# Low parts, decays and an ELU step change engines and tiles while float64 weights are narrowed

## The chip, the core and the metric

The kernel runs on one core of one Trainium2 chip. The core has five engines that run their own instruction lists in order: TensorE (PE in the profile, with its weight loads as PEld), VectorE (DVE), ScalarE (ACT), GpSimd (POOL) and SyncE (SP, which here only starts transfers). They meet at semaphores. The metric is the device time of one execution in microseconds (us), as the median of several runs.

## The reference, cut to what matters

Three stages follow each other: retention attention with a decay per head, a dense feed-forward layer with ELU, and a routed feed-forward layer with eight experts.

```python
for t in range(S):                                   # B=4, H=8, S=768, D=64
    state = gamma * state + einsum('bhd,bhe->bhde', k[:, :, t], v[:, :, t])
    y[:, :, t] = scale * einsum('bhd,bhde->bhe', q[:, :, t], state)
h = x @ w_in                                         # 3072x512 @ 512x2048, w_in is float64
g = np.where(h > 0.0, h, np.exp(np.minimum(h, 0.0)) - 1.0)
x2 = (g @ w_out).astype(np.float32)                  # 2048x512, w_out is float64
...
logits = x2 @ w_gate                                 # then a greedy assignment, 384 tokens per expert
out[mask] = np.maximum(x2[mask] @ w1[e], 0.0) @ w2[e]
```

## The kernel before, in words

**Attention in units.** The tokens are cut into 24 units: one batch and one chunk of 128 tokens each, chunk 0 of all four batches first (units 0 to 3), then chunk 1 (units 4 to 7), and so on. Per unit SP loads `qk` and `kv`; `decays` multiplies the queries by `gq` (a power of gamma that rises with the token) and the values by `gk` (the inverse power); PE computes the scores `sc`; `masks` multiplies them by the triangle `tri` into `A`; `attend` forms `py` from A and the values, and for later chunks from the state `st`; `carry` forms `pu` from keys and values and VectorE adds it to `st`. `y_out` splits `py` into a high part `yH` (ACT) and a low part `yL` (VectorE).

**Blocks.** Two units make a block of 256 tokens, numbered n from 0 to 11. For a block and each of 8 slices i of the hidden layer PE computes the first product `ph` (24 matmuls, named phn_i below), and ACT and VectorE turn it into ELU: ACT forms Relu(-h) and Exp of its negative in `e`, then 1 is subtracted, then VectorE takes max(h, 0) + e. ACT and VectorE (or POOL) split it into `gH` and `gL`, and PE accumulates the second product `px` (12 matmuls for a slice). Every product uses three passes, high x high, high x low, low x high.

**Weights.** w_in and w_out arrive as float64 in 16 slices of two pieces (`rw`, 512 KB each); the order of the slices is w1 0, w1 1, w2 0, w1 2, w2 1, and so on. Per piece `scales` multiplies the upper words (ACT mostly), `narrow` builds a float32 out of the two words in three VectorE instructions over a tile `n_rw` (shift left, and/or, shift right/or), `highs` rounds it into `w1H` or `w2H` on ACT, and `lows` subtracts that into `w1L` or `w2L`. Before the change the third narrowing step writes into `rw` itself, with a stride of two words, and the high and low steps read it there.

**Order.** No loop sets the order. Each of these functions is a generator that names, ahead of each instruction, the engine or a choice of engines with a cost in ns, the tiles it needs and a condition; a planner with its own clock for each engine repeatedly takes the instruction that can start first, with ranks to break ties, and emits it. What an engine executes is therefore one fixed list. The first weights are needed by block 0 and 1 while they are narrowed. Once all lows are out, the weight stage's tiles are released, the gate weights `wgb` are loaded into their place, and VectorE gets a further load that fills its gaps: `junk` (dot products of finished rows with the gate weights) and `junkw` (the same with summed weights `wsum`). Routing and the experts follow after the last block.

All engine calls pass through one wrapper, so the profile gives nearly every instruction the line L201; tiles tell them apart.

Of the kernel before, what the change touches and what calls it, by code (L numbers as in the profile page):

```python
# [18 lines left out]
OP = mybir.AluOpType  # L19
# [30 lines left out]
def _constants():  # L50
# [10 lines left out]
    tri = (t[:, None] <= t[None, :]).astype(np.float64)  # L61
    gk = gam[None, :] ** (-(t[:, None] + 1.0))
# [226 lines left out]
def body(ctx: ExitStack, tc, qkv, w_in, w_out, w_gate_t, w1, w2, cst, rc, rmat, out, dbg=None):  # L289
# [68 lines left out]
    def decays():  # L358
        for k in range(len(seq)):
            yield on({"DVE": 600 + DEC, "POOL": 1050}, csb, when=lambda: did["unit_load"] > k)  # L360
            u = units[k]
            eng = yield on({"DVE": 600 + DEC, "POOL": 1050}, u["q0"])
            engines[eng].tensor_tensor(u["q0"], u["q0"], gq, op=OP.mult)
# [15 lines left out]
    def scores(k):  # L379
# [6 lines left out]
        yield on("PE", bank_slot(spare_tag()), csb, when=lambda: did["decay_q"] > k)  # L386
# [8 lines left out]
    def masks(k):  # L395
        u = units[k]
        u["A"] = []
        for hh in range(2):
            yield on("DVE", u["sc"][hh], ap.slot(f"A{hh}", 1))
            a = ap.tile([P, NP, P], F32, tag=f"A{hh}", bufs=1, name=f"A{k}_{hh}")  # L400
            DVE.tensor_tensor(a, u["sc"][hh].rearrange("p (a b) -> p a b", a=NP), tri, op=OP.mult)
            u["A"].append(a)

    def attend(k):
        b, c = seq[k]
        yield on("PE", bank_slot(spare_tag()), when=lambda: did["decay"] > k)
# [50 lines left out]
    def attention():  # L457
        ahead = False
        for k in range(len(seq)):
# [3 lines left out]
            ahead = k < 3 and did["decay_q"] > k + 1  # L463
# [9 lines left out]
    stage[1] = Tiles(stage[0].enter_context(tc.tile_pool(name="stg", bufs=2)), plan, 2)  # L473
    win, wout, raws, slim = {}, {}, {}, {}
# [47 lines left out]
    def narrow():  # L522
        for s, (nm, i) in enumerate(slices):
            group = [[0], [1]] if s == 0 else [[0, 1]]
            for cs in group:
                yield on("DVE", when=lambda: did["scaled"] > 2 * s + cs[-1] if wide else did["weight"] > s)
# [14 lines left out]
                for c, r in zip(cs, rs):  # L541
                    slim[(nm, i, c)] = words(r, 0).bitcast(F32)
# [69 lines left out]
    def elus(par):  # L612
        for k in range(par, n_all, 2):
# [707 lines left out]
```

## Time and profile before

| what | value |
|---|---|
| median of 3 runs | 1062.28 us (1062.04 to 1063.79) |
| the profiled execution's own time | 1063.49 us |
| its span in the trace | 1061.7 us, mean granted TensorE clock 0.967 |
| busy: PE / DVE / ACT / POOL | 984.9 / 773.2 / 395.2 / 234.6 us |

The own time is the one the device reports for the profiled execution; the span reaches from its first to its last recorded instruction. Busy time of an engine counts instructions only, including the time that a started instruction is held up. The granted clock is 1.00 at 2.4 GHz and lower where a stretch was partly run at 1.2 GHz.

### The profile page before, as it was taken

How to read it: one execution, taken by the hardware profiler on the slowest of the kernel's cores; microseconds unless marked ns; L12 is line 12 of the kernel's file. 1: busy time of each engine (PE TensorE's matmuls, PEld its weight loads, DVE VectorE, ACT ScalarE, POOL GpSimd, SP SyncE). 2: the span in 40 equal slices, each digit the busy share in tenths (PEclk: the TensorE clock that was granted, in tenths of full speed). 3: DMA queues.
4: the chain of work that ended last, by engine and by line, in shares of the span. 5: the costliest groups of instructions: out<-in, count | busy, mean ns of one | idle time of the engine just before them, and what ended most of it. 6: DMA issues, size and time to landing. Idle time of an engine off the chain costs nothing.

```text
span 1061.7 us, 17628 instructions
## 1 busy us (share of the span) xinstructions
PE 984.9 (93%) x6899; PEld 846.8 (80%) x6899; DVE 773.2 (73%) x1876; ACT 395.2 (37%) x614; POOL 234.6 (22%) x220
## 2 busy tenths in 40 slices
PE   4586999998999999999999999995999999999996
PEld 4475888887888888888888889874878878888995
DVE  4999876998898989894647475557868778877320
ACT  2454423332332332323333334403354453445541
POOL 2557521111112221120201000001041132233221
PEclk9788999999999999899999999997999999999998
DMA  9762141111110303030201000006577677668850
GB/s 312 275 223 75 40 179 61 40 60 41 47 53 5 96 2 99 2 100 1 101 1 61 1 21 2 12 21 211 154 210 199 189 203 214 178 193 248 232 138 34
DMA packets 55971, 115.01 MB, mean 108 GB/s; under 512 B 4176, under 2 KB 28752, under 8 KB 55760
## 3 DMA queue, kind: packets, MB, share of 16 engines
q1 hardware_dynamic: 47440, 84.52, 24.0%
q0 software_dynamic: 8448, 29.37, 11.6%
q8 instruction: 54, 0.88, 0.3%
q14 instruction: 29, 0.24, 0.1%
HBM read 84.51 MB, written 12.58 MB: 91 GB/s over the span
## 4 chain that ended last, share of the span: by engine, by line
PE 63%; DVE 23%; issue 8%; DMA 2%; POOL 2%; ACT 2%; SPq 0%; POOLq 0%; DVEq 0%; ACTq 0%
PE px L201 19%; PE ph L201 17%; PE po L201 9%; PE eh L201 9%; DVE junk L201 6%; DVE n_rw L201 5%; DVE e L201 3%; DVE junkw L201 3%; PE py L201 2%; PE sc L201 2%; DVE gL L201 2%; DVE rw L201 2%; DMA xg<-xd,idx 1%; DVE A L201 1%; PE pt L201 1%
## 5 line engine op out<-in xcount | busy, mean ns | idle before, releaser
L201 PE MATMUL ph<-yH,w1H 128*128 128x256 f32 x768 | 222.9, 290 | 18.8 <-DVE e L201 18.3
L201 PE MATMUL ph<-yH,w1L 128*128 128x256 f32 x768 | 219.1, 285 | 1.9 <-POOL w1L L201 1.9
L201 PE MATMUL ph<-yL,w1H 128*128 128x256 f32 x768 | 218.8, 285 | 0.3 <-DVE yL L201 0.3
L201 PEld LDWEIGHTS ph<-yH,w1H 128*128 128x128 f32 x768 | 148.5, 193 | 24.8 <-DVE e L201 14.3
L201 PEld LDWEIGHTS ph<-yH,w1L 128*128 128x128 f32 x768 | 148.6, 193 | 4.0 <-POOL w1L L201 2.5
L201 PEld LDWEIGHTS ph<-yL,w1H 128*128 128x128 f32 x768 | 148.8, 194 | 0.5 <-DVE yL L201 0.5
L201 PE MATMUL px<-w2H,gH 128*128 128x512 f32 x332 | 135.9, 409 | 4.8 <-ACT gH L201 4.8
L201 PE MATMUL px<-w2H,gL 128*128 128x512 f32 x332 | 132.4, 399 | 4.1 <-DVE gL L201 4.1
L201 DVE SCALAR_TENSOR_TENSOR junk<-x,wgb 128x512 f32<-128x512 f32 x160 | 131.6, 822 | 5.4 <-ACT x L201 1.2
L201 PE MATMUL px<-w2L,gH 128*128 128x512 f32 x332 | 132.4, 399 | 0.0
L201 ACT ACTIVATE e<-ph 128x512 f32<-128x512 f32 x96 | 56.7, 591 | 175.4 <-PE ph L201 174.7
L201 ACT ACTIVATE gH<-e 128x512 fp32r<-128x512 f32 x83 | 52.4, 631 | 122.5 <-DVE e L201 116.7
L201 DVE SCALAR_TENSOR_TENSOR junkw<-wsum,wgb 128x512 f32<-128x512 f32 x128 | 90.2, 705 | 10.5 <-POOL wsum L201 8.3
L201 PE MATMUL eh<-xTL,w1H 128*128 128x384 f32 x256 | 89.2, 349 | 0.5 <-DVE xTL L201 0.5
L201 PE MATMUL eh<-xTH,w1H 128*128 128x384 f32 x256 | 89.7, 350 | 0.0
L201 PE MATMUL eh<-xTH,w1L 128*128 128x384 f32 x256 | 88.1, 344 | 0.0
L201 PEld LDWEIGHTS px<-w2H,gH 128*128 128x128 f32 x332 | 63.2, 190 | 21.9 <-ACT gH L201 5.7
L201 ACT ACTIVATE hH<-eh 128x384 fp32r<-128x384 f32 x64 | 31.3, 490 | 131.0 <-PE eh L201 118.7
L201 PEld LDWEIGHTS px<-w2H,gL 128*128 128x128 f32 x332 | 63.1, 190 | 21.3 <-DVE gL L201 6.2
L201 PE MATMUL po<-w2H,hL 128*128 128x512 f32 x192 | 77.6, 404 | 0.0
L201 PE MATMUL po<-w2H,hH 128*128 128x512 f32 x192 | 77.5, 404 | 0.0
L201 PE MATMUL po<-w2L,hH 128*128 128x512 f32 x192 | 77.4, 403 | 0.0
(170 smaller groups left out, 1847.2 us busy)
## 6 DMA issues: line engine op xcount, KB each, us to landing
e1R<-in_w_dram SPq DMA_DIRECT2D x32, 512.0 KB, 6.5
e2R<-in_w_dram SPq DMA_DIRECT2D x32, 512.0 KB, 4.5
kv<-in_qkv_dram SPq DMA_DIRECT2D x24, 512.0 KB, 5.4
qk<-in_qkv_dram SPq DMA_DIRECT2D x23, 512.0 KB, 5.3
rw<-in_moe_w_in_dram SPq DMA_DIRECT2D x16, 512.0 KB, 10.4
rw<-in_moe_w_out_dram SPq DMA_DIRECT2D x16, 512.0 KB, 8.7
w1L<-e1R POOLq DMA_DIRECT2D x16, 512.0 KB
w2L<-e2R POOLq DMA_DIRECT2D x16, 512.0 KB
```

Of the source, the lines that this page charges most:

```text
L201: r = real(*args, **kw)
```

## The change

Four edits. (1) `lows` runs on VectorE alone, and `scales` may use ACT or VectorE only, and the list that results holds no POOL arithmetic before the decays of unit 8. (2) `decays`: for the first 8 units only VectorE may do it; units of chunk 0 get no decay of the queries at all. Their scores are multiplied by `hmask` instead, a mask per head that holds the triangle times the power of gamma (512 KB, loaded as one transfer), and their values are decayed only after `attend` has read them, for the state. `csb`, which holds gq, gk and tri, is loaded after the first unit. (3) The third narrowing step writes into `n_rw`, which gets four buffers and a condition on finished lows. (4) The subtraction of 1 and the maximum of the ELU become one VectorE instruction, max(e - 1, h).

```diff
+BUSY = 8
+NAR = 4
...
-DEC, LOW = 500, 900
+DEC = 500
...
 def load_units():
             if k == 0:
+                SP.dma_start(hmask, hm)
             SP.dma_start(kv, qkv[b, c][:, 2:])
+            if k == 0:
+                SP.dma_start(csb, cst)
+                SP.dma_start(rcs, rc)
...
 def decays():
-            yield on({"DVE": 600 + DEC, "POOL": 1050}, csb, when=lambda: did["unit_load"] > k)
+            engs = {"DVE": 600} if k < BUSY else {"DVE": 600 + DEC, "POOL": 1050}
+            yield on(engs, csb, when=lambda: did["unit_load"] > k)
+            if c > 0:
+                eng = yield on(engs, u["q0"])
                 engines[eng].tensor_tensor(u["q0"], u["q0"], gq, op=OP.mult)
-            eng = yield on({"DVE": 600 + DEC, "POOL": 1050}, u["v"])
+            eng = yield on(engs, u["v"], when=lambda: c > 0 or did["attended"] > k)
             engines[eng].tensor_tensor(u["v"], u["v"], gk[:, :, None].to_broadcast([P, H, D]), op=OP.mult)
...
 def masks(k):
+            mask = tri if seq[k][1] else hmask[:, hh * NP * P : (hh + 1) * NP * P].rearrange("p (a b) -> p a b", a=NP)
-            DVE.tensor_tensor(a, u["sc"][hh].rearrange("p (a b) -> p a b", a=NP), tri, op=OP.mult)
+            DVE.tensor_tensor(a, u["sc"][hh].rearrange("p (a b) -> p a b", a=NP), mask, op=OP.mult)
...
 def scales():
-                eng = yield on({"ACT": 900, "DVE": 900, "POOL": 1230}, g)
+                eng = yield on({"ACT": 600, "DVE": 600}, g)
...
 def narrow():
+                    and did["low", "w1"] + did["low", "w2"] > 2 * s + cs[-1] - NAR,
-                        o = stage[1].tile(list(r.shape)[:-1], U32, tag="nar", name=f"n_{r.name}")
+                        o = stage[1].tile(list(r.shape)[:-1], U32, tag="nar", bufs=NAR, name=f"n_{r.name}")
-                        DVE.scalar_tensor_tensor(words(r, 0), words(r, 0), 29, o, op0=OP.logical_shift_right, op1=OP.bitwise_or)
+                        DVE.scalar_tensor_tensor(o, words(r, 0), 29, o, op0=OP.logical_shift_right, op1=OP.bitwise_or)
...
 def lows():
-                yield on("POOL", when=lambda: did["high"] > 2 * s + c)
+                yield on("DVE", when=lambda: did["high"] > 2 * s + c)
-                eng = yield on({"POOL": 1230, "DVE": 600 + LOW}, hi)
-                engines[eng].tensor_sub(lo, slim.pop((nm, i, c)), hi.bitcast(F32))
+                DVE.tensor_sub(lo, slim.pop((nm, i, c)), hi.bitcast(F32))
...
 def elus(par):
-            eng = yield on({"ACT": 520, "DVE": 340}, e)
-            if eng == "ACT":
-                ACT.activation(e, e, AF.Copy, bias=-1.0)
-            else:
-                DVE.tensor_scalar(e, e, -1.0, None, op0=OP.add)
             yield on("DVE", e)
-            DVE.scalar_tensor_tensor(e, ph, 0.0, e, op0=OP.max, op1=OP.add)
+            DVE.scalar_tensor_tensor(e, e, -1.0, ph, op0=OP.add, op1=OP.max)
```

Since the planner writes the lists anew, the order changes too. Three places follow; in the names rw100 is slice 0 of w1, piece 0 (rw2 is w2), the figure after sc, py, pu, A, qk and kv is the unit, and the last number only tells buffers apart.

VectorE at the start of the weight stage, from the first narrowing on. Before:

```order
L201 SCALAR_TENSOR_TENSOR n_rw100_93_141<-rw100_93,n_rw100_93_141 128x512
L201 SCALAR_TENSOR_TENSOR rw100_93<-rw100_93,n_rw100_93_141 128x512
L201 TENSOR_SCALAR n_rw101_95_159<-rw101_95 128x512
L201 TENSOR_TENSOR yL0_157<-py0_138,yH0_156 128x4x128
L201 TENSOR_TENSOR st_78<-pu0_165,csb_77 128x256
L201 TENSOR_TENSOR A1_0_181<-sc1_0_126,csb_77 128x512
L201 TENSOR_TENSOR A1_1_183<-sc1_1_127,csb_77 128x512
L201 SCALAR_TENSOR_TENSOR n_rw101_95_159<-rw101_95,n_rw101_95_159 128x512
L201 SCALAR_TENSOR_TENSOR rw101_95<-rw101_95,n_rw101_95_159 128x512
L201 TENSOR_SCALAR n_rw110_97_198<-rw110_97 128x512
L201 TENSOR_SCALAR n_rw111_99_200<-rw111_99 128x512
L201 TENSOR_TENSOR yL0_157<-py1_185,yH0_156 128x4x128
```

VectorE in the changed kernel, from the lows of the second slice to the same yL of unit 1:

```order
L208 TENSOR_TENSOR w1L_1_207<-n_rw110_101_190,w1H_1_206 128x4x128
L208 TENSOR_TENSOR w1L_1_207<-n_rw111_103_193,w1H_1_206 128x4x128
L208 TENSOR_SCALAR n_rw120_109_237<-rw120_109 128x512
L208 TENSOR_SCALAR n_rw121_111_241<-rw121_111 128x512
L208 SCALAR_TENSOR_TENSOR n_rw120_109_237<-rw120_109,n_rw120_109_237 128x512
L208 SCALAR_TENSOR_TENSOR n_rw121_111_241<-rw121_111,n_rw121_111_241 128x512
L208 TENSOR_TENSOR kv1_94<-kv1_94,csb_77 128x512
L208 SCALAR_TENSOR_TENSOR n_rw120_109_237<-rw120_109,n_rw120_109_237 128x512
L208 TENSOR_TENSOR yL0_147<-py1_239,yH0_146 128x4x128
```

The yL of unit 1, which completes the input of block 0, stood in VectorE's list behind two narrowed pieces; now it stands behind six, four lows and two decays of values.

PE ahead of the first product ph0_0 (repeated rows of a group left out). Before:

```order
L201 MATMUL pu0_165<-kv0_85 64x64 x8
L201 MATMUL py1_185<-A1_0_181,kv1_90 64x128
L201 MATMUL py1_185<-A1_1_183,kv1_90 64x128
...
L201 MATMUL pu1_204<-kv1_90 64x64 x8
L201 MATMUL ph0_0_220<-yH0_156,w1H_0_161 128x256
L201 MATMUL ph0_0_220<-yH0_156,w1L_0_162 128x256
L201 MATMUL ph0_0_220<-yL0_157,w1H_0_161 128x256
```

PE in the changed kernel, at the same place:

```order
L208 MATMUL pu0_153<-kv0_84 64x64 x8
L208 MATMUL sc2_0_172<-qk2_163 128x128
L208 MATMUL sc2_1_173<-qk2_163 128x128
...
L208 MATMUL py1_239<-A1_0_167,kv1_94 64x128
L208 MATMUL py1_239<-A1_1_169,kv1_94 64x128
...
L208 MATMUL ph0_0_258<-yH0_146,w1H_0_183 128x256
L208 MATMUL ph0_0_258<-yH0_146,w1L_0_184 128x256
L208 MATMUL pu1_261<-kv1_94 64x64 x8
L208 MATMUL ph0_0_258<-yL0_147,w1H_0_183 128x256
```

The scores of unit 2, whose load qk2 stands in SP's queue behind the first eight weight pieces, now come ahead of py of unit 1, and the first product is split around pu of unit 1.

VectorE at the first ELU. Before:

```order
L201 TENSOR_SCALAR e0_0_284<-e0_0_284 128x512
L201 SCALAR_TENSOR_TENSOR rw120_105<-rw120_105,n_rw120_105_274 128x512
L201 SCALAR_TENSOR_TENSOR e0_0_284<-ph0_0_220,e0_0_284 128x512
L201 SCALAR_TENSOR_TENSOR rw121_107<-rw121_107,n_rw121_107_280 128x512
L201 TENSOR_SCALAR n_rw210_152_332<-rw210_152 128x512
L201 TENSOR_TENSOR gL0_0_327<-e0_0_284,gH0_0_326 128x512
```

And in the changed kernel:

```order
L208 SCALAR_TENSOR_TENSOR e0_0_313<-e0_0_313,ph0_0_258 128x512
L208 SCALAR_TENSOR_TENSOR n_rw210_176_326<-rw210_176,n_rw210_176_326 128x512
L208 SCALAR_TENSOR_TENSOR n_rw211_178_332<-rw211_178,n_rw211_178_332 128x512
L208 TENSOR_TENSOR gL0_0_344<-e0_0_313,gH0_0_343 128x512
L208 SCALAR_TENSOR_TENSOR n_rw210_176_326<-rw210_176,n_rw210_176_326 128x512
```

One VectorE instruction of each ELU is gone; what stands between e and gL is narrowing in both.

## Rows read from the trace of the kernel before

**Rows 1.** The page, busy time, share of the span and instructions of each engine.

```profile
PE 984.9 (93%) x6899; PEld 846.8 (80%) x6899; DVE 773.2 (73%) x1876; ACT 395.2 (37%) x614; POOL 234.6 (22%) x220
```

**Rows 2.** Windows: length, busy of PE, PEld, DVE, ACT, POOL, clock, DMA share, GB/s.

```profile
15.38:17.26 1.88, 1.88 (x22) 1.88 (x24) 1.81 (x4) 0.68 (x1) 0.00 (x0) 1.00 1.11 374
...
22.00:188.05 166.05, 138.61 (x1053) 118.29 (x1053) 144.32 (x218) 71.35 (x121) 75.86 (x50) 0.90 0.42 148
...
45.00:67.00 22.00, 17.89 (x136) 14.59 (x136) 22.00 (x37) 12.55 (x21) 5.98 (x5) 0.89 0.52 167
...
188.05:688.00 499.95, 486.87 (x3652) 430.25 (x3653) 383.01 (x824) 167.84 (x280) 67.08 (x57) 0.99 0.12 39
```

**Rows 3.** DVE's groups between 15 and 125 us: busy us, mean ns | idle before.

```profile
L201 DVE SCALAR_TENSOR_TENSOR n_rw<-rw,n_rw 128x512 uint32<-128x512 uint32 x31 | 30.8, 1020 | 0.0
L201 DVE TENSOR_SCALAR n_rw<-rw 128x512 uint32<-128x512 uint32 x32 | 26.1, 840 | 4.6 <-ACT rw L201 4.0 <-POOL rw L201 0.6
L201 DVE SCALAR_TENSOR_TENSOR rw<-rw,n_rw 128x512 uint32<-128x512 uint32 x30 | 22.7, 777 | 0.1
L201 DVE TENSOR_TENSOR gL<-e,gH 128x512 fp32r<-128x512 f32 x8 | 9.1, 1143 | 1.7 <-ACT gH L201 1.7
L201 DVE TENSOR_SCALAR e<-e 128x512 f32<-128x512 f32 x7 | 6.2, 882 | 0.0
L201 DVE SCALAR_TENSOR_TENSOR e<-ph,e 128x512 f32<-128x512 f32 x9 | 6.1, 679 | 0.2
...
L201 DVE TENSOR_TENSOR w2L<-rw,w2H 128x512 fp32r<-128x512 f32 x2 | 1.3, 679 | 0.0
```

**Rows 4.** Timeline of POOL, then DVE, near 70 us: start, length, instruction.

```profile
69.07 1.23 POOL L201 TENSOR_TENSOR kv<-kv,csb 128x512 f32<-128x512 f32 x1
70.26 1.74 POOL L201 TENSOR_TENSOR w1L<-rw,w1H 128x512 fp32r<-128x512 f32 x1
...
69.31 1.53 DVE L201 SCALAR_TENSOR_TENSOR n_rw<-rw,n_rw 128x512 uint32<-128x512 uint32 x1
70.77 1.79 DVE L201 TENSOR_TENSOR gL<-e,gH 128x512 fp32r<-128x512 f32 x1
```

**Rows 5.** Timeline of DVE at two moments at which POOL runs nothing.

```profile
15.38 0.43 DVE L201 TENSOR_SCALAR n_rw<-rw 128x512 uint32<-128x512 uint32 x1 [4.01 <-ACT rw L201]
...
46.96 0.68 DVE L201 SCALAR_TENSOR_TENSOR rw<-rw,n_rw 128x512 uint32<-128x512 uint32 x1
47.56 0.68 DVE L201 TENSOR_TENSOR gL<-e,gH 128x512 fp32r<-128x512 f32 x1
...
49.37 0.41 DVE L201 TENSOR_SCALAR n_rw<-rw 128x512 uint32<-128x512 uint32 x1
49.70 1.28 DVE L201 TENSOR_TENSOR w2L<-rw,w2H 128x512 fp32r<-128x512 f32 x2
```

**Rows 6.** ACT's longest wait between 15 and 125 us: us, times, longest.

```profile
ACT w1H L201 <- DVE rw L201: 23.0, 8, 5.8
```

**Rows 7.** Pieces of the chain that ended last: start, length, what.

```profile
151.95 8.40 PE px L201 x36
160.35 8.43 PE ph L201 x72
168.78 1.09 PE sc L201 x16
...
172.87 2.04 PE py L201 x32
...
177.90 0.61 PE pu L201 x16
...
253.53 4.62 PE ph L201 x24
```

**Rows 8.** Timeline of PE: the start of ph2_2, block 2, slice 2.

```profile
187.96 0.39 PE L201 MATMUL ph<-yH,w1H 128*128 128x256 f32 x1
```

**Rows 9.** PE's waits between 130 and 680 us: us, times, longest.

```profile
PE ph L201 <- DVE e L201: 12.9, 7, 2.9
```

More of the change, by code (lines that the diff above doesn't have):

```diff
@@ L61, in _constants @@
     tri = (t[:, None] <= t[None, :]).astype(np.float64)
+    hm = np.zeros((P, 2, NP, P))
+    for pr in range(NP):
+        for hh in range(2):
+            hm[:, hh, pr] = tri * gam[2 * pr + hh] ** np.maximum(t[None, :] - t[:, None], 0) / math.sqrt(D)
     gk = gam[None, :] ** (-(t[:, None] + 1.0))
@@ L81, in _constants @@
     return {
+        "hm": np.ascontiguousarray(hm.reshape(P, -1).astype(np.float32)),
         "cst": np.ascontiguousarray(cst),
@@ L358, in decays @@
     def decays():
-        for k in range(len(seq)):
-            yield on({"DVE": 600 + DEC, "POOL": 1050}, csb, when=lambda: did["unit_load"] > k)
+        for k, (b, c) in enumerate(seq):
+            engs = {"DVE": 600} if k < BUSY else {"DVE": 600 + DEC, "POOL": 1050}
+            yield on(engs, csb, when=lambda: did["unit_load"] > k)
             u = units[k]
-            eng = yield on({"DVE": 600 + DEC, "POOL": 1050}, u["q0"])
-            engines[eng].tensor_tensor(u["q0"], u["q0"], gq, op=OP.mult)
+            if c > 0:
+                eng = yield on(engs, u["q0"])
+                engines[eng].tensor_tensor(u["q0"], u["q0"], gq, op=OP.mult)
             did["decay_q"] += 1
-            eng = yield on({"DVE": 600 + DEC, "POOL": 1050}, u["v"])
+            eng = yield on(engs, u["v"], when=lambda: c > 0 or did["attended"] > k)
             engines[eng].tensor_tensor(u["v"], u["v"], gk[:, :, None].to_broadcast([P, H, D]), op=OP.mult)
@@ L385, in scores @@
             spare["tags"] = ("at", "at")
-        yield on("PE", bank_slot(spare_tag()), csb, when=lambda: did["decay_q"] > k)
+        yield on("PE", bank_slot(spare_tag()), *([csb] if seq[k][1] else []), when=lambda: did["decay_q" if seq[k][1] else "unit_load"] > k)
         u = units[k]
@@ L405, in attend @@
         b, c = seq[k]
-        yield on("PE", bank_slot(spare_tag()), when=lambda: did["decay"] > k)
+        yield on("PE", bank_slot(spare_tag()), when=lambda: c == 0 or did["decay"] > k)
         u = units[k]
@@ L437, in carry @@
             u = units[k]
-            yield on("PE", bank_slot(spare_tag()))
+            yield on("PE", bank_slot(spare_tag()), u["v"], when=lambda: did["decay"] > k)
             pu = spare_bank(f"pu{k}")
@@ L462, in attention @@
             yield from masks(k)
-            ahead = k < 3 and did["decay_q"] > k + 1
+            ahead = k < 3 and did["unit_load"] > k + 1
             if ahead:
@@ L473, in body @@
     stage[1] = Tiles(stage[0].enter_context(tc.tile_pool(name="stg", bufs=2)), plan, 2)
+    hmask = stage[1].tile([P, 2 * NP * P], F32, tag="hm", bufs=1, name="hmask")
     win, wout, raws, slim = {}, {}, {}, {}
@@ L512, in scales @@
             for c in range(2):
-                yield on({"ACT": 900, "DVE": 900, "POOL": 1230}, when=lambda: did["weight"] > s)
+                yield on({"ACT": 600, "DVE": 600}, when=lambda: did["weight"] > s)
                 g = words(raws[(nm, i, c)], 1).bitcast(F32)
-                eng = yield on({"ACT": 900, "DVE": 900, "POOL": 1230}, g)
+                eng = yield on({"ACT": 600, "DVE": 600}, g)
                 if eng == "ACT":
@@ L525, in narrow @@
             for cs in group:
-                yield on("DVE", when=lambda: did["scaled"] > 2 * s + cs[-1] if wide else did["weight"] > s)
+                yield on(
+                    "DVE",
+                    when=lambda: (did["scaled"] > 2 * s + cs[-1] if wide else did["weight"] > s)
+                    and did["low", "w1"] + did["low", "w2"] > 2 * s + cs[-1] - NAR,
+                )
                 rs = [raws.pop((nm, i, c)) for c in cs]
@@ L539, in narrow @@
                         yield on("DVE", o)
[L540 to L542 removed]
+                        DVE.scalar_tensor_tensor(o, words(r, 0), 29, o, op0=OP.logical_shift_right, op1=OP.bitwise_or)
+                for c, r in zip(cs, tmp if wide else rs):
+                    slim[(nm, i, c)] = r.bitcast(F32) if wide else words(r, 0)
                     did["narrow"] += 1
```

9 lines of the change are left out of this document (5 added, 4 removed).

## Prediction

> **What bounds the kernel now.** The page comes first: TensorE is busy for 93% of the span and VectorE for 73% [rows 1], so time can be won only where TensorE waits or runs at the low clock. The windows show where that is. From 188 to 688 us TensorE is busy for 486.87 of 499.95 us at a clock of 0.99; from 22 to 188 us it is busy for 138.61 of 166.05 us at 0.90 [rows 2]. That second stretch is the weight stage and what it leaves behind. How much it loses can be counted. Its end, 187.96 us, is the start of ph2_2 [rows 8]; up to there, from 22 us on, TensorE executes 18 first products, 17 second products, and the scores, py and pu of units 2 to 8. The chain prices them at the full clock [rows 7]: a first product is 8.43/3 = 2.81 us, a second 8.40/3 = 2.80, scores 1.09, py 2.04 (half of it in chunk 0, which has no state), pu 0.61. That makes 50.6 + 47.6 + 24.1 = about 122 of 166 us; 44 us are lost, 27 in idle time and the rest to the low clock.
>
> VectorE is what it waits for. In this stretch VectorE is busy without gaps for long times (22.00 of 22.00 us from 45 to 67 us), and ACT waits for narrowed weights, 23.0 us in 8 waits [rows 2, 6]. The groups of VectorE then show that it is slowed and not only loaded. A narrowing step of one form takes 1020 ns on average and another 840 [rows 3], while single ones take 0.68 and 0.41 to 0.43 us when POOL does nothing [rows 5]. The timeline says how: at 69 and 70 us two instructions with both inputs in SBUF last 1.53 and 1.79 us, next to POOL instructions of 1.23 and 1.74 us [rows 4]. The ELU's maximum, which reads one input from PSUM, keeps its 679 ns over the whole stage [rows 3]. Transfers are not the reason: at 15.4 us they run at 374 GB/s, POOL is idle, and VectorE's step takes 0.43 us [rows 2, 5].
>
> The Trainium skill, page "SBUF — State Buffer", section "Who interferes with whom", says the same of these forms: VectorE instructions with two SBUF inputs or in a two-port mode exclude GpSimd instructions for their whole length, those with one SBUF input do not. The trace agrees (1.53 against 0.68 us, and 679 ns unmoved).
>
> **The change part by part.**
>
> *POOL's arithmetic goes.* Taking 0.68 us for large instructions and 0.42 for two-port ones as free lengths, the excess between 15 and 125 us is 30.8 - 31 x 0.68 = 9.7 for the and/or step, 26.1 - 32 x 0.42 = 12.7 for the shift, 22.7 - 30 x 0.68 = 2.3 for the last step, 9.1 - 8 x 0.68 = 3.7 for gL and 6.2 - 7 x 0.42 = 3.3 for the ELU's subtraction [rows 3, 5]: 31.7 us.
>
> *VectorE takes over.* It gets 29 lows more (its list had 3 of the 32) and, up to the last low, 10 decays (3 of queries, 7 of values). One that follows another costs the distance of starts, 0.60 us (46.96 to 47.56), a short one 0.33 (49.37 to 49.70) [rows 5]. That is 17.4 + 6.0 us. The fused ELU step saves 0.33 for each of 7 subtractions in the stage, 2.3. Balance: 31.7 + 2.3 - 23.4 = 10.6 us shorter for the same work.
>
> *The start.* hmask puts 512 KB ahead of the first weights; at 374 GB/s [rows 2] that is 1.4 us. VectorE's first narrowing, at 15.38 us [rows 5], moves to 16.8. The earlier scores of unit 0 gain nothing, since VectorE waits for weights then.
>
> *The new list, summed.* From the first narrowing to the last low, VectorE's new list has 146 large instructions (64 narrowing, 32 lows, 8 A, 10 decays, 5 yL, 14 ELU, 13 gL) and 40 short ones: 146 x 0.60 + 40 x 0.34 = 101 us, so to 118 us if it never waits. The four n_rw buffers cost no wait: lows of a slice stand behind the narrowing of the next, six instructions or about 3 us, in which ACT has two roundings of 0.68 us (its row for one instruction at 15.4 us [rows 2]) to do. Against that stands the start of TensorE. Unit 1's yL is now behind 17 us of VectorE's list plus about 0.5 us where steps of one tile follow each other; ph0_0 can go on only at 16.8 + 17.5 + 0.7 = 35 us. The scores of unit 2 ahead of it wait for a load behind eight weight pieces; the first piece is there at 15.4 - 0.7 + 1.4 = 16 us, so that load at 16 + 8 x 1.4 = 27 us, which is earlier and hidden.
>
> *TensorE from 35 us.* Up to the start of ph2_2 the new list holds 18 first and 18 second products (px2_1 now comes before ph2_2), and about 23.6 us of unit work: 50.6 + 50.4 + 23.6 = 125 us, that is to 160 us without loss. Followed row by row with the prices above, the two lists wait for each other at few places. ph0_0 starts cold: 4.62 instead of 2.81 us after an idle time [rows 7], 1.8 us. px0_0 waits 1.4 us for ELU and gL; the py of unit 3 waits 2.0 us for its A, which stands behind pu of unit 2 and the decay that must follow py of unit 2; the input of block 1 costs 1.5. From about 57 us VectorE's deliveries lead by 1 to 2 us. For the low clock I take 45 to 67 us as a pattern (0.89, so 11% of 22 us, 2.4 us [rows 2]). Dots ahead of the A of unit 8 add 1. Sum 10, so ph2_2 starts at 170 us. Before, with px2_1 added, it was at 187.96 + 2.8 = 190.8. **Gain 21 us**; 31 without any loss, 9 (10.6 - 1.4) if TensorE only follows the shortening of VectorE's own work.
>
> *The later ELUs.* Between 130 and 680 us PE waits 7 times, 12.9 us, for e, and restarts at half clock, 4.62 us for a product [rows 7, 9]. Each late e stands behind dots in VectorE's list; one instruction less ahead of it is 0.42 us and its gap, say 0.5. 7 x 0.5 = **4 us**. From below this is 0 (the planner fills the gap with more dots), from above 13 plus 5 of low clock.
>
> *Elsewhere.* Decays of units 8 to 23, dots, routing and experts keep their work; the lists there are shuffled by a few instructions, worth nothing here and 3 us either way in the range. The stage's release of tiles, at about 123 us, lets the gate weights arrive while VectorE still waits for TensorE.
>
> Sum: 25 us. The profiled execution took 1063.5 us, 1.8 over its span and 1.2 over the median of the runs, so 1038.5 by its own time and 1037 against the median of 1062.3.
>
> The Trainium skill, page "Perfetto Trace Analysis", section "Optimizing Scalar/DVE Operations", speaks against the change: with VectorE saturated, work may be handed to Scalar or even GpSimd. By that rule alone 23.4 us come back to the bound engine and the kernel gets slower. The same section warns of the shared read port; rows 4 show that this warning decides here.
>
> **The rivals.**
>
> *Only VectorE's own saving.* TensorE starves as often as before, since it begins 13 us later, and gains the 9 us by which VectorE's work shrinks: 1053. For it: two engines at 101 and 125 us of work in one stretch wait for each other often, and each idle time brings the low clock. Against: the new list has both blocks' products interleaved with the narrowing, so TensorE has work ready from about 57 us.
>
> *More than that.* The waits cancel and late ELUs no longer stall PE: 31 + 13 = 44, about 1020. Against: the planner prices a dot at 0.60 us, as any large instruction, and the dots stay.
>
> *Slower: lows block VectorE.* Narrowing and lows now form one in-order list with ACT's rounding in between. If ACT is held up by its own ELU work, everything behind a low waits, narrowing included. There are 16 pairs of lows; at 1.6 us each the 25 us are gone, at 2.5 us (two roundings and two ELU steps) it is 40 us and 1077. Against: ACT is busy for 12.55 of 22 us and waits for VectorE, not the reverse [rows 2, 6].
>
> *Slower: POOL is not the cause.* If the long instructions stay long, 31.7 us return: ph2_2 at 202 instead of 190.8, and 1069 with the later saving. Rows 4 and 5 speak against it.
>
> *No change:* the gain is lost again in later waits, 1062. The tail from 188 us is 97% busy, so little there can absorb it.
>
> **How the numbers follow.** Forecast 0.62, only VectorE's saving 0.17, more 0.11, the two slower ones 0.07 together, none 0.03. The forecast's own range is 1028 to 1047. The range of 8 in 10 reaches to 1025 and 1054. About 0.2% can be told from no change: faster 0.90, same 0.03, slower 0.07.
>
> **What would show it.** Narrowing steps near 0.42 and 0.68 us on average; VectorE's list to the last low ending near 120 us; ph0_0 near 35 us; TensorE nearly full from 60 us; ph2_2 near 170 us, and the same distance from there to the end, less some 4 us. Wrong would be lows that wait for ACT by more than a microsecond, a clock below 0.85 between 35 and 120 us, or more PE waits for e after 190 us.

## The result and the profile after

The changed kernel takes 1034.39 us, median of 4 runs (1032.64 to 1037.57), against 1062.16 us for the kernel before, also 4 runs (1059.38 to 1063.79) on the same chip. The ratio is 0.9731 with a 95% interval of 0.9703 to 0.9759: 28 us, or 2.7%, faster. The forecast was 1037 us. The profiled execution took 1035.3 us, with a span of 1033.5 us.

The page of the kernel after, in the line that answers to [rows 1]:

```profile
PE 975.4 (94%) x6899; PEld 839.4 (81%) x6899; DVE 730.2 (71%) x1843; ACT 389.8 (38%) x603; POOL 151.0 (15%) x164
```

TensorE executes the same 6899 matmuls in a shorter span. Windows of the kernel after (columns as in [rows 2]); the last reaches from the start of ph2_2 to the first `pl`, the matmul that opens routing:

```profile
22.00:188.05 166.05, 153.11 (x1195) 133.59 (x1196) 148.71 (x287) 76.78 (x130) 9.25 (x7) 0.98 0.44 154
45.00:67.00 22.00, 20.00 (x211) 17.26 (x211) 19.88 (x37) 11.58 (x20) 0.00 (x0) 0.92 0.53 186
169.18:656.10 486.92, 478.19 (x3633) 422.59 (x3629) 353.92 (x762) 161.34 (x268) 58.73 (x51) 1.00 0.12 40
```

In the same 166 us TensorE is now busy for 153 instead of 139, at a clock of 0.98 instead of 0.90, and VectorE is no longer full between 45 and 67 us. The groups of VectorE between 15 and 130 us (columns as in [rows 3]) say why:

```profile
L208 DVE SCALAR_TENSOR_TENSOR n_rw<-rw,n_rw 128x512 uint32<-128x512 uint32 x64 | 41.2, 684 | 0.1
L208 DVE TENSOR_SCALAR n_rw<-rw 128x512 uint32<-128x512 uint32 x32 | 12.6, 419 | 0.0
L208 DVE TENSOR_TENSOR w2L<-n_rw,w2H 128x512 fp32r<-128x512 f32 x16 | 10.5, 684 | 0.0
L208 DVE TENSOR_TENSOR w1L<-n_rw,w1H 128x512 fp32r<-128x512 f32 x16 | 10.5, 683 | 0.0
...
L208 DVE TENSOR_TENSOR gL<-e,gH 128x512 fp32r<-128x512 f32 x14 | 9.6, 687 | 2.1 <-ACT gH L208 1.8
L208 DVE TENSOR_TENSOR kv<-kv,csb 128x512 f32<-128x512 f32 x7 | 4.8, 688 | 8.0 <-PE py L208 6.5 <-DMA kv<-in_qkv_dram 1.5
```

Every form has the length that [rows 5] show where GpSimd runs nothing: 684 ns for the second and third narrowing steps, which now share a row (1020 and 777 before); 419 for the shift, 840 before; 687 for gL, 1143 before. The 32 lows wait for nothing (idle 0.0). PE's timeline shows the start of ph2_2, which answers to [rows 8]:

```profile
169.18 0.39 PE L208 MATMUL ph<-yH,w1H 128*128 128x256 f32 x1
```

The span before can be cut at the same two places, ph2_2 and the first `pl`, here from the views of `pl` before and after:

```profile
L201 PE MATMUL pl<-rcs,ls x8: 251/251/272, 686.4 to 687.2; 16*128 16x8 f32 x8
```

```profile
L208 PE MATMUL pl<-rcs,ls x8: 251/251/272, 656.1 to 656.9; 16*128 16x8 f32 x8
```

Up to ph2_2, with the px2_1 that now stands ahead of it: 187.96 + 2.8 - 169.18 = 21.6 us won. From there to `pl`: 686.4 - 190.8 = 495.6 before, 486.9 after, 8.7 won. From `pl` to the end: 375.3 before, 377.4 after, 2.1 lost. Together 28.2 us, the difference of the spans. The window before that answers to the last row above:

```profile
190.80:686.40 495.60, 482.52 (x3621) 426.01 (x3619) 379.95 (x816) 167.20 (x279) 66.25 (x53) 0.99 0.12 38
```

Two new waits came with the change. VectorE's timeline at the start, then TensorE's at ph0_0, and then PE's longest waits between 17 and 170 us (us, times, longest):

```profile
15.57 0.69 DVE L208 TENSOR_TENSOR kv<-kv,csb 128x512 f32<-128x512 f32 x1 [6.21 <-PE py L208]
16.18 0.42 DVE L208 TENSOR_SCALAR n_rw<-rw 128x512 uint32<-128x512 uint32 x1
...
19.02 1.41 DVE L208 SCALAR_TENSOR_TENSOR n_rw<-rw,n_rw 128x512 uint32<-128x512 uint32 x2
...
32.46 0.68 DVE L208 TENSOR_TENSOR kv<-kv,csb 128x512 f32<-128x512 f32 x1
33.06 0.68 DVE L208 SCALAR_TENSOR_TENSOR n_rw<-rw,n_rw 128x512 uint32<-128x512 uint32 x1
33.66 0.68 DVE L208 TENSOR_TENSOR yL<-py,yH 128x512 fp32r<-128x512 f32 x1
```

```profile
31.21 0.58 PE L208 MATMUL ph<-yH,w1H 128*128 128x256 f32 x1 [1.49 <-ACT yH L208]
...
34.39 0.58 PE L208 MATMUL ph<-yL,w1H 128*128 128x256 f32 x1
```

```profile
PE sc L208 <- DMA qk<-in_qkv_dram: 8.2, 1, 8.2
PE ph L208 <- ACT yH L208: 2.2, 2, 1.5
```

The values of unit 0 may be decayed only after py of unit 0, and this decay stands ahead of the first narrowing in VectorE's list: VectorE waits 6.21 us for it. TensorE waits 8.2 us for the load of unit 2, whose scores now come ahead of py of unit 1. VectorE does not wait behind that: from 16.18 us to the end of the yL of unit 1, at 34.34, it is busy for 17.80 of 18.16 us. The first two matmuls of ph0_0 start at 31.21 us; the third, which reads this yL, starts at 34.39 us.

### The profile page after: what moved, and what is told of

It is laid out like the page before. It is cut to its first block, busy times and chain, and to the rows that moved or that the text cites. A ratio compares the mean times of both kernels' runs of the same rounds, so it can differ in the third digit from the quotient of the medians.

```text
span 1033.5 us, 17471 instructions
## 1 busy us (share of the span) xinstructions
PE 975.4 (94%) x6899; PEld 839.4 (81%) x6899; DVE 730.2 (71%) x1843; ACT 389.8 (38%) x603; POOL 151.0 (15%) x164
## 4 chain that ended last, share of the span: by engine, by line
PE 74%; DVE 11%; issue 7%; DMA 3%; ACT 2%; POOL 1%; POOLq 0%; SPq 0%; DVEq 0%; ACTq 0%
PE px L208 23%; PE ph L208 22%; PE po L208 10%; PE eh L208 10%; DVE junk L208 5%; PE py L208 3%; PE sc L208 2%; DMA xg<-xd,idx 2%; DVE junkw L208 2%; DVE gL L208 1%; PE pt L208 1%; DVE e L208 1%; PE pu L208 1%; PE lacc L208 1%; PE pc L208 1%
## 5 line engine op out<-in xcount | busy, mean ns | idle before, releaser
L208 PE MATMUL ph<-yH,w1H 128*128 128x256 f32 x768 | 220.3, 287 | 12.4 <-DVE e L208 10.2
L208 PE MATMUL ph<-yL,w1H 128*128 128x256 f32 x768 | 216.4, 282 | 0.1
L208 PE MATMUL ph<-yH,w1L 128*128 128x256 f32 x768 | 216.2, 281 | 0.0
L208 PEld LDWEIGHTS ph<-yH,w1H 128*128 128x128 f32 x768 | 146.0, 190 | 18.3 <-DVE e L208 12.1
L208 PEld LDWEIGHTS ph<-yH,w1L 128*128 128x128 f32 x768 | 146.0, 190 | 1.2
L208 PEld LDWEIGHTS ph<-yL,w1H 128*128 128x128 f32 x768 | 146.0, 190 | 0.4 <-DVE yL L208 0.3
L208 DVE SCALAR_TENSOR_TENSOR junk<-x,wgb 128x512 f32<-128x512 f32 x160 | 128.1, 801 | 5.1 <-ACT x L208 1.2
L208 DVE SCALAR_TENSOR_TENSOR e<-e,ph 128x512 f32<-128x512 f32 x96 | 65.6, 684 | 56.8 <-ACT e L208 56.7
L208 DVE TENSOR_TENSOR gL<-e,gH 128x512 fp32r<-128x512 f32 x83 | 64.4, 776 | 22.4 <-ACT gH L208 21.1
```

Of the source, the lines that this page charges most:

```text
L208: r = real(*args, **kw)
```

## The experiments

All variants are compared with the kernel before on the same chip; the ratio and its interval stand with each. A ratio of 0.01 is 10.6 us. "Up to pl" is the start of the first `pl` in the profile; the rest of the span has no edit in any variant.

**Is it GpSimd beside VectorE? Unused sums.** Behind each low GpSimd adds the high part to itself into a tile that nobody reads. The lists of the other engines stay as they are.

```diff
                 DVE.tensor_sub(lo, slim.pop((nm, i, c)), hi.bitcast(F32))
+                for h in range(2):
+                    src = ...                        # 240 columns of hi
+                    nc.gpsimd.tensor_tensor(scr, src, src, op=OP.add)
```

> The kernel after, with work added that nobody reads: behind each of the 32 lows GpSimd adds the high part to itself into an unused tile, in two instructions of 128x240. VectorE's, ScalarE's and TensorE's lists stay the same, row for row, so VectorE neither gains nor loses an instruction. Theory (GpSimd's arithmetic lengthens VectorE's instructions with two inputs in SBUF and its two-port shift): 64 instructions of about 0.65 us, by 1.23 us for 512 columns in rows 4, keep GpSimd busy for 42 us of the stage, against 65.7 us before (the trace: 42 instructions); in proportion VectorE's excess is 31.7 x 42 / 65.7 = 20 us; narrowing steps rise to about 0.60 (shift) and 0.85 us (and/or), ph2_2 comes 12 to 20 us later than 169.2, time 1046 to 1055. Rival (the time came from the new order of the list and from what leaves it, and GpSimd beside it costs nothing): narrowing steps at 0.42 and 0.68 us, 1031 to 1038.

Measured: 1049.64 us, ratio 0.9884 (0.9868 to 0.9901), which is 15 us slower than the kernel after; ph2_2 starts at 183.8 us, 14.6 later, and `pl` at 670.3, 14.2 later. GpSimd's groups and VectorE's between 15 and 150 us in this variant:

```profile
L594 POOL TENSOR_TENSOR scrap<-w2H 128x240 bf16<-128x240 f32 x32 | 32.1, 1004 | 36.7 <-ACT w2H L208 34.9
L594 POOL TENSOR_TENSOR scrap<-w1H 128x240 bf16<-128x240 f32 x32 | 24.5, 766 | 49.0 <-ACT w1H L208 47.3
...
L208 DVE SCALAR_TENSOR_TENSOR n_rw<-rw,n_rw 128x512 uint32<-128x512 uint32 x64 | 45.8, 753 | 0.1
L208 DVE TENSOR_SCALAR n_rw<-rw 128x512 uint32<-128x512 uint32 x32 | 17.9, 586 | 0.0
L208 DVE TENSOR_TENSOR w1L<-n_rw,w1H 128x512 fp32r<-128x512 f32 x16 | 14.8, 949 | 0.0
L208 DVE TENSOR_TENSOR w2L<-n_rw,w2H 128x512 fp32r<-128x512 f32 x16 | 13.3, 856 | 0.0
L208 DVE SCALAR_TENSOR_TENSOR e<-e,ph 128x512 f32<-128x512 f32 x15 | 10.2, 678 | 2.5 <-ACT e L208 2.5
```

The excess over the lengths of the kernel after is 64 x 0.069 + 32 x 0.167 + 16 x 0.266 + 16 x 0.172 = 16.8 us, and 1.5 more in gL and the decays: 18 us for 56.6 us of GpSimd. The ELU step, with one input in PSUM, keeps its 678 ns. With VectorE's list untouched, GpSimd's arithmetic alone takes away half of what the change won. The rival (order and number of instructions, and GpSimd costs nothing) is out; that order has a part in the rest is not excluded.

**One input instead of two.** As above, with a copy.

```diff
-                    nc.gpsimd.tensor_tensor(scr, src, src, op=OP.add)
+                    nc.gpsimd.tensor_copy(scr, src)
```

> As the run with GpSimd's unused sums, but each of the 64 unused GpSimd instructions is a copy with one input instead of a sum with two. Theory (any GpSimd access to SBUF excludes such VectorE instructions, and the excess goes with the time GpSimd is busy): 64 copies of 0.4 to 0.65 us, 26 to 42 us busy, excess 13 to 20 us, time 1042 to 1055. Rival (only GpSimd instructions that read two inputs disturb VectorE): 1031 to 1038, narrowing at 0.42 and 0.68 us.

Measured: 1040.64 us, ratio 0.9798 (0.9780 to 0.9817), 6 us slower than the kernel after; ph2_2 at 173.5, `pl` at 660.1. Between 15 and 140 us:

```profile
L594 POOL CAST scrap<-w2H 128x240 bf16<-128x240 f32 x32 | 19.6, 612 | 35.5 <-ACT w2H L208 34.0
L594 POOL CAST scrap<-w1H 128x240 bf16<-128x240 f32 x32 | 18.4, 575 | 57.0 <-ACT w1H L208 55.7
...
L208 DVE SCALAR_TENSOR_TENSOR n_rw<-rw,n_rw 128x512 uint32<-128x512 uint32 x64 | 43.5, 718 | 0.1
L208 DVE TENSOR_SCALAR n_rw<-rw 128x512 uint32<-128x512 uint32 x32 | 15.5, 513 | 0.0
```

Copies disturb too, so the rival falls; but less than expected, and the time lies between the two ranges. The excess is 8.5 us, worked out as above (w1L 796, w2L 757, gL 709 ns), for 38.0 us of GpSimd: 0.22 us for each us of GpSimd, against 18.3/56.6 = 0.32 with sums. A cost "per us of GpSimd" is thus not one number.

**The lows back on GpSimd.** Only this part of the change is undone.

```diff
-                yield on("DVE", hi)
-                DVE.tensor_sub(lo, slim.pop((nm, i, c)), hi.bitcast(F32))
+                eng = yield on({"POOL": 1230, "DVE": 1500}, hi)
+                engines[eng].tensor_sub(lo, slim.pop((nm, i, c)), hi.bitcast(F32))
```

> The kernel after with one part undone: the lows may go to GpSimd again, at the planner's old prices; mask per head, own decays on VectorE and the fused ELU stay. Theory: VectorE loses up to 29 lows (17.4 us) and gets back an excess of about 29 x 1.6 us of GpSimd work x 31.7/65.7 = 22 us, so it is about as busy as in the kernel after or 5 us more; but TensorE can begin earlier (yL of unit 1 is no longer behind lows): 1033 to 1045. Rival 1 (GpSimd beside VectorE costs nothing): VectorE's list is 17 us shorter, 1018 to 1028. Rival 2 (the lows were the whole cost): back near the kernel before less the ELU's 9 us, 1050 to 1056.

Measured: 1059.63 us, ratio 0.9974 (0.9956 to 0.9992): 15 us above the top of what was expected, and above the second rival. VectorE behaves as the theory says, between 15 and 130 us:

```profile
L208 DVE SCALAR_TENSOR_TENSOR n_rw<-rw,n_rw 128x512 uint32<-128x512 uint32 x64 | 52.4, 854 | 0.1
L208 DVE TENSOR_SCALAR n_rw<-rw 128x512 uint32<-128x512 uint32 x32 | 22.7, 740 | 0.6 <-POOL w2L L208 0.6
```

The excess is 64 x 0.170 + 32 x 0.321 = 21.2 us, 3.3 more for 7 decays and 1.4 for 9 gL: 26 instead of 22. Its last and/or step starts at 118.6 us, against 121.1 in the kernel after, so VectorE is not later. TensorE is: 84.6 us busy between 15 and 130 us, against 99.2. The expectation took TensorE's start from VectorE alone. ScalarE's timeline shows what it missed:

```profile
31.06 1.23 ACT L208 ACTIVATE w2H<-n_rw 128x512 fp32r<-128x512 f32 x2 [3.00 <-DVE n_rw L208]
36.28 1.23 ACT L208 ACTIVATE w1H<-n_rw 128x512 fp32r<-128x512 f32 x2 [3.99 <-DVE n_rw L208]
37.42 0.58 ACT L208 ACTIVATE yH<-py 128x512 fp32r<-128x512 f32 x1
```

yH of unit 1, which ph0_0 needs, stands behind two roundings that wait for lengthened narrowing; PE waits 9.2 us for it, and ph0_0 starts at 38.05 instead of 31.21. Later it waits 4.95 us ahead of a py at 68.97, for a reason the profile doesn't name. So without the lows' part of the change 0.9974 - 0.9731, or 26 us, are gone; in the profiles 18.9 of it lie up to `pl` (675.0). The planner wrote another list here too, so how much of the 26 us is GpSimd's and how much is order (yH behind the roundings) is not shown.

**The fused ELU step alone, on the kernel before.**

```diff
-            eng = yield on({"ACT": 520, "DVE": 340}, e)
-            ...                                      # subtract 1 there
-            DVE.scalar_tensor_tensor(e, ph, 0.0, e, op0=OP.max, op1=OP.add)
+            DVE.scalar_tensor_tensor(e, e, -1.0, ph, op0=OP.add, op1=OP.max)
```

> The kernel before with the fused ELU step alone; lows, decays and masks as before. Theory by the prediction's terms: 2.3 us off VectorE in the stage and 0.5 us for each of 7 late e behind it, 4 us: 1055 to 1058. By what the kernel after gained behind ph2_2 (8.7 us) if all of that is the ELU: 1050 to 1053. Rival (the fused step saves nothing where other work is planned into its place): 1061 to 1063.

Measured: 1057.04 us, ratio 0.9949 (0.9930 to 0.9967), 5 us, in the range of the prediction's terms, but not by them: ph2_2 starts no earlier (188.6 us), where 2.3 us were expected; `pl` does, by 9.5, where these and 4 more were; and the tail behind it gives 3.3 back. PE's waits for e fall from 12.9 to 7.6 us.

**The kernel after without the fused step** (the same lines, in reverse).

> The kernel after with the ELU in its two old steps again (subtraction of 1, then maximum and sum). Theory: 2.3 us more for VectorE in the weight stage (7 subtractions at 0.33 us), and the 8.7 us that were gained behind ph2_2 go, of which 4 were forecast: 1039 to 1045. Rival (the gain behind ph2_2 is a side effect of the earlier stage): 1034 to 1037.

Measured: 1047.15 us, ratio 0.9839 (0.9799 to 0.9879), some 11 us over the kernel after by the ratios; the median is 2 us past the expected range. ph2_2 starts 4.9 us later (174.1), `pl` 10.9 (667.0). PE's waits between 170 us and `pl`, in this variant, and in the kernel after, where they answer to [rows 9]:

```profile
PE ph L208 <- DVE e L208: 16.7, 10, 2.8
```

```profile
PE ph L208 <- DVE e L208: 8.6, 7, 2.5
```

Up to `pl` the step is worth about the same in both kernels, 9.5 and 10.9 us; that the whole times differ by 5 and by 11 us comes mostly from the tail, which this edit does not touch. What differs is the place: in the kernel after 4.9 us of it lie ahead of ph2_2, in the kernel before none.

**Dearer dots.** The planner's clock for VectorE is moved on by 170 ns more at each dot. It is a change of the order only.

```diff
         DVE.scalar_tensor_tensor(junk, src, 1.0, wgb[:, e, :], op0=OP.mult, op1=OP.mult, accum_out=acc)
+        plan.free["DVE"] += 170.0
```

> The kernel after, with the planner's clock for VectorE advanced by 170 ns more at each gate dot, so that it puts fewer dots ahead of an ELU step; the work is the same, and so is TensorE's list. PE still waits 7 times, 8.6 us, for e between 170 and 660 us. Theory (late e's stand behind dots that take longer than planned): 3 to 7 of the 8.6 us go, with restarts at the low clock: 1026 to 1031. Rival (they are late for another reason, such as ScalarE's exponential or the banks): 1033 to 1036.

Measured: 1029.21 us, ratio 0.9672 (0.9636 to 0.9707). The same view:

```profile
PE ph L208 <- DVE e L208: 4.8, 7, 1.2
```

From ph2_2 to `pl` it takes 480.4 instead of 486.9 us, of which 3.8 are waits. The rest is lower clock that is saved: in the chain of the kernel after the product behind the wait of 2.52 us at 177.62 takes 4.52 us, here the one at 173.77, behind 0.18 us, takes 3.09. The late e did stand behind dots.

**No scores of unit 2 ahead.**

```diff
-            ahead = k < 3 and did["unit_load"] > k + 1
+            ahead = k < 1 and did["unit_load"] > k + 1
```

> The kernel after, with one condition of the order changed: only the scores of unit 1 are moved ahead of the unit before, those of units 2 and 3 are not. In the trace of the kernel after TensorE waits 8.2 us from 25.65 us on for the load of unit 2, with py of unit 1 queued behind it; py, yL of unit 1 and ph0_0 wait with it. Theory: py of unit 1 no longer waits, ph0_0 comes up to 8 us earlier, and as TensorE is nearly full from 57 us on, 3 to 6 us of it reach the end: 1028 to 1032. Rival 1 (VectorE's list sets the pace up to the last low, and TensorE then waits later for it): 1033 to 1036. Rival 2 (the list is shuffled for the worse): over 1037.

Measured: 1029.79 us, ratio 0.9663 (0.9619 to 0.9708). ph0_0 starts at 22.00 instead of 31.21 us, and its matmul that needs yL of unit 1 at 24.18 instead of 34.39, since the planner now puts this yL at 20.83 us of VectorE's list, ahead of most of the narrowing it stood behind. Of these 10 us 2.2 are left at `pl` in the profile: ph0_0 starts before the low parts are there (1.21 and 1.69 us of waits for w1L), and until 31 us its matmuls follow each other at 0.21 instead of 0.12 us, the low clock.

**No mask per head.** The queries and values of chunk 0 are decayed on VectorE ahead of use, as before; `hmask` and its load go; the scores of unit 2 then come behind py of unit 1 as well.

```diff
-            if c > 0:
+            if True:
                 eng = yield on(engs, u["q0"])
...
-            eng = yield on(engs, u["v"], when=lambda: c > 0 or did["attended"] > k)
+            eng = yield on(engs, u["v"])
...
-            mask = tri if seq[k][1] else hmask[...]
+            mask = tri
...
-            ahead = k < 3 and did["unit_load"] > k + 1
+            ahead = k < 3 and did["decay_q"] > k + 1
```

> The kernel after with the decays of chunk 0 done by VectorE on the queries and on the values ahead of use, as before, instead of in a mask per head: four more instructions on VectorE (0.60 us each), no load of 512 KB ahead of the weights, constants loaded first. By the prediction's terms: 4 x 0.6 = 2.4 us more on VectorE, 1.4 us won at the start: 1034 to 1037. Theory: within 3 us of the kernel after either way, 1032 to 1038. Rival (decays at the very start hold up the first y, since they wait for the constants and the loads): 1038 to 1045.

Measured: 1023.81 us, ratio 0.9621 (0.9586 to 0.9657). This is faster than the kernel after, by 0.0110 or 12 us, and all three ranges missed it. VectorE's timeline at the start, to be read against the one of the kernel after:

```profile
14.07 0.43 DVE L208 TENSOR_SCALAR n_rw<-rw 128x512 uint32<-128x512 uint32 x1 [1.54 <-ACT rw L208]
14.53 0.69 DVE L208 SCALAR_TENSOR_TENSOR n_rw<-rw,n_rw 128x512 uint32<-128x512 uint32 x1
```

The second narrowing step starts at 14.53 instead of 19.02 us, py of unit 1 at 17.79 instead of 27.75, ph0_0 at 20.11 instead of 31.21; `pl` starts at 647.9, 8.2 earlier. Three runs look for the part that does it.

**No mask, but the scores of unit 2 ahead again** (`ahead` as in the kernel after).

> The version with the first chunk's decays on VectorE again, but with the scores of unit 2 ahead of py of unit 1, as in the kernel after; that version alone had moved them behind it. Theory (of its 10.6 us, 4.6 are the order, by the run in which the order alone was changed, and 6 the mask: with it the decay of the values must wait for py of its own unit, 6.2 us, and VectorE's first narrowing behind it): 1027 to 1030. Rival 1 (all of it is the order): 1032 to 1036. Rival 2 (all of it is the mask): 1022 to 1025.

Measured: 1033.81 us, ratio 0.9738 (0.9713 to 0.9762), as slow as the kernel after, as the rival said by which all of it is the order. PE waits 14.67 us ahead of the scores of unit 2, here for their decay on VectorE; `pl` at 653.0, which is still 3.1 us earlier than in the kernel after.

**No mask, but its 512 KB still loaded** and not used.

```diff
             if k == 0:
+                SP.dma_start(hmask, hm)
```

> The version with the first chunk's decays on VectorE again, with the 512 KB of the mask per head still loaded ahead of the weights, and not used. It separates the transfer from the wait for py. Theory (the wait is what costs; the transfer costs 1.4 us at 374 GB/s): 1024 to 1027. Rival (the start is set by the transfer): 1029 to 1033.

Measured: 1033.91 us, ratio 0.9734 (0.9711 to 0.9757), also as slow as the kernel after, where the theory said 1024 to 1027. But the transfer does not stand alone: here the planner also wrote another list: unit 1's scores behind py of unit 0, and the first narrowing behind the A of unit 1, at 18.67 us. `pl`, however, starts at 649.4, only 1.5 later than without the load; the other 6.3 us of the profiled spans lie behind `pl`, where nothing was edited. The windows from `pl` to the end, of the version without the load and then of this one:

```profile
647.90:1025.40 377.50, 352.97 (x2111) 293.72 (x2110) 240.50 (x826) 150.31 (x203) 86.20 (x109) 0.97 0.61 171
```

```profile
649.40:1033.20 383.80, 356.60 (x2111) 294.98 (x2110) 237.65 (x823) 150.32 (x206) 87.19 (x109) 0.96 0.60 168
```

The same 2111 matmuls take 3.6 us more of busy time, and 2.7 more is idle.

**No mask, with the dearer dots.**

> The version with the first chunk's decays on VectorE again (1023.8 us) and the dearer gate dots (5.2 us won on the kernel after) together. Theory (the first acts up to about 40 us, by an earlier start of narrowing and an earlier py of unit 1; the second behind 170 us, on late e's, so they add): 1023.8 - 5.2 = 1018 to 1021. Rival (both take from the same waits for e, 8.6 us after, 4.8 with dearer dots, 7.7 with the old mask): 1022 to 1025.

Measured: 1022.26 us, ratio 0.9624 (0.9607 to 0.9641): the lowest median, and by its ratio no faster than without the dearer dots. `pl` starts 4.5 us earlier (643.4) and PE still waits 6.9 us for e, in place of 7.7. The rival holds: the two gains are not added.

**No mask, decays of the first 7 units on GpSimd.**

```diff
-            engs = {"DVE": 600} if k < BUSY else {"DVE": 600 + DEC, "POOL": 1050}
+            engs = {"DVE": 600 + DEC, "POOL": 1050}
```

> The version with all decays before use and no mask per head (1023.8 us), with the decays of the first 7 units on GpSimd again, 14 instructions; the lows stay on VectorE and the ELU fused. It asks whether the weight stage wants GpSimd empty or only rid of the lows. Theory (the excess goes with GpSimd's busy time, and the lows were most of it): VectorE loses 14 x 0.60 = 8.4 us; 14 x 1.25 to 1.5 us = 17 to 21 us of GpSimd bring an excess of 31.7 x 19 / 65.7 = 9 us, so VectorE is even; decays on GpSimd take twice as long, 0.6 to 0.8 us more in each unit's chain, of which 0 to 5 us show: 1023 to 1029. Rival 1 (any GpSimd arithmetic in the stage is dear, as 15 us for 49 us of it in the run with unused sums): 19/49 x 15 = 6, less nothing for VectorE's relief: 1029 to 1034. Rival 2 (VectorE's relief counts more, since the decays stand early where GpSimd meets few two-input instructions): 1018 to 1022.

Measured: 1031.45 us, ratio 0.9692 (0.9661 to 0.9723), about 8 us slower than with the decays on VectorE. It is the time of the first rival, but not quite by its mechanism: VectorE's narrowing steps are hardly lengthened (688 and 448 ns), its w2L and gL somewhat (833 and 799 ns, 4 us together). GpSimd is lengthened more: the ten decays from 29.36 us on take 25.4 us in all. Its timeline, and then VectorE's beside it:

```profile
6.30 1.26 POOL L208 TENSOR_TENSOR qk<-qk,csb 128x512 f32<-128x512 f32 x1 [5.84 <-DMA qk<-in_qkv_dram]
...
29.36 6.11 POOL L208 TENSOR_TENSOR qk<-qk,csb 128x512 f32<-128x512 f32 x1 [15.36 <-DMA qk<-in_qkv_dram]
...
64.58 7.29 POOL L208 TENSOR_TENSOR qk<-qk,csb 128x512 f32<-128x512 f32 x1 [6.12 <-DMA qk<-in_qkv_dram]
```

```profile
64.47 0.68 DVE L208 SCALAR_TENSOR_TENSOR n_rw<-rw,n_rw 128x512 uint32<-128x512 uint32 x1
65.07 0.41 DVE L208 TENSOR_TENSOR st<-st,csb 128x256 f32<-128x256 f32 x1
65.41 1.28 DVE L208 TENSOR_TENSOR w1L<-n_rw,w1H 128x512 fp32r<-128x512 f32 x2
66.61 0.41 DVE L208 TENSOR_SCALAR n_rw<-rw 128x512 uint32<-128x512 uint32 x1
66.95 0.68 DVE L208 TENSOR_TENSOR gL<-e,gH 128x512 fp32r<-128x512 f32 x1
67.55 0.41 DVE L208 TENSOR_SCALAR n_rw<-rw 128x512 uint32<-128x512 uint32 x1
67.89 2.48 DVE L208 SCALAR_TENSOR_TENSOR n_rw<-rw,n_rw 128x512 uint32<-128x512 uint32 x4
70.29 0.42 DVE L208 TENSOR_SCALAR rw<-rw 128x512 f32<-128x512 f32 x1
70.63 0.67 DVE L208 SCALAR_TENSOR_TENSOR e<-e,ph 128x512 f32<-128x512 f32 x1
71.23 2.65 DVE L208 TENSOR_TENSOR w2L<-n_rw,w2H 128x512 fp32r<-128x512 f32 x2
```

The decay that starts at 64.58 us ends at 71.87. VectorE's instructions keep their free lengths until 70.63 us; then comes an ELU step, which reads PSUM, and behind it two lows take 2.65 us instead of 1.28. TensorE waits 3.5 us for decays on GpSimd between 17 and 130 us. How the 8 us come about is open: `pl` of the profiled execution, the fastest of its six runs, starts at 648.4, only 0.5 us later than with the decays on VectorE.

Two parts of the change were not undone alone: the third narrowing step with its four buffers, and the bar on GpSimd for `scales`.

## Why the prediction was right, point by point

*What bounds.* VectorE's lengthened instructions starved TensorE between 22 and 188 us. Shown: all forms fell to the free lengths that were read from [rows 5], and putting unused sums back on GpSimd brought 15 of the 28 us back.

*VectorE's balance.* The lows cost their 0.60 us each and no wait; ahead of the decays of values VectorE stood idle for 8.0 us, 6.2 of them at the very start. The list to the last low was put at 118 us, 123 with waits; the last two lows end at 125.5.

*The start.* First narrowing forecast at 16.8 us, measured at 16.18; but not for the reason given, so this number is luck. The 1.4 us of the transfer do not show: ScalarE scales the first piece at 14.32 us, against 14.69 in the kernel before, and without the mask it does so at 13.36 in one run and at 14.63 in another. What moves the narrowing is the first decay, which waits 6.21 us for py of unit 0, and the second narrowing step came only at 19.02. The prediction saw that such a decay "must follow py" for unit 2 and not for unit 0.

*ph0_0.* Forecast to go on at 35 us, measured at 34.39, and by the path forecast: VectorE needs 17.5 us from its first narrowing to the start of yL of unit 1, almost without a gap. The load of unit 2, put at 27 us, was there at 25.65; TensorE waited 8.2 us for it, but this stayed hidden behind VectorE's list, as forecast. What the prediction took as given was the order itself: another order gave 0.9663 instead of 0.9731, with intervals that just meet.

*ph2_2.* Forecast at 170 us, a gain of 21; measured 169.18 and 21.6. The 10 us of loss behind 35 us came out in sum (134.8 us from 34.39 us on, for 125 us of work) but not in parts: TensorE is idle for about 4.0 us, where the listed waits make 5.9, and the low clock takes the other 5.8, where 4.2 were put.

*Later ELUs.* Right in kind, too small: "7 x 0.5 = 4 us" measured 8.7. The waits themselves fell by 4.3 us, from 12.9 to 8.6 [rows 9], as the term had it; from ph2_2 to `pl` TensorE's idle time fell by 4.4 us and its busy time for the same products by 4.3, from 482.5 to 478.2. This second half, the product that runs at the low clock behind a wait, the prediction named but put only into its upper bound. Undoing the fused step alone cost about 11 us, 4.9 of it up to ph2_2, where the balance had 2.3. The late e's cause, dots ahead of it, held in the run with dearer dots.

*Elsewhere.* Forecast 0, within 3; measured 2.1 lost. The sum, 25 us, was 3 too small: the ELU term missed 4.7, ph2_2 0.6, and the tail took 2.1 back.

*The rivals.* "Lows block VectorE" did not come: the lows' idle time is 0.0. "POOL is not the cause" is refuted by the unused sums. The Trainium skill, page "Perfetto Trace Analysis", section "Optimizing Scalar/DVE Operations", says that a saturated VectorE may hand work to GpSimd, but that it might not help. Here it cost time: 0.9974 against 0.9731 with the lows on GpSimd, and 0.9692 against 0.9621 with 14 decays there.

*What it did not see.* The mask per head was costed at 1.4 us, and the version without it, with another order, is about 12 us faster. With either the transfer or the early scores of unit 2 put back the gain is gone in the whole time, but neither run isolates a cause: the planner's list changed in both. Up to `pl` they account for 1.5 and 5.1 of 8.2 us, and why the tail behind it differs by 2 to 6 us is not settled.

## What to carry to other kernels

Price an engine's instruction by what it does to its neighbour: here GpSimd's instructions beside VectorE's with two SBUF inputs made one of the two late (1020 instead of 684 ns, or 6.11 instead of 1.26 us), and moving the work to VectorE at its plain price won even where VectorE was the bound. Before an operation is moved behind another engine's result (here the decay behind py), look at what stands behind it in its own list at the very start. And undo every part of a combined change on its own: on the kernel after, the lows were worth 26 us, the fused step 11, and the mask with its order cost 12; these do not simply add, since each undoing also changes the list.

## What was not expected of the hardware

Who pays is not fixed. In the kernel before VectorE's instructions were stretched ([rows 4]); with the decays alone on GpSimd, VectorE mostly ran on undisturbed, and one form of GpSimd instruction that took 1.26 us at 6.30 us, when VectorE had little to do, took 6.11 and 7.29 us. Both times it ended about 1.2 us after VectorE had begun an ELU step, which has an input in PSUM (at 34.26 and 70.63 us), so it seems to have run only then. The Trainium skill, page "SBUF — State Buffer", section "Who interferes with whom", says of VectorE's two-port modes that whoever issues first gets the shared pair for the whole instruction. The trace agrees in kind, and shows more: a stream of twelve VectorE instructions without a gap, most of them with two inputs in SBUF, from 64.47 to 70.63 us, kept the other out throughout.

Copies on GpSimd, with one input, stretched VectorE's shift from 419 to 513 ns and its and/or step from 684 to 718; sums to 586 and 753.

The stretch from `pl` to the end, with the same work in all kernels, took between 375.3 and 383.8 us in their profiles. Differences of a few us between single profiles therefore say nothing about an edit ahead of it.
